# The phases of a head pair in another order: three score tiles, half the values, three groups of turning

## The chip, the cores and the metric

The kernel runs on one core of a Trainium2 chip. What counts is the device time of one execution in microseconds (us). The engines are named TensorE (PE in the rows), VectorE (DVE), ScalarE (ACT), GpSimd (POOL) and SyncE (SP, which here issues most DMAs).

## The reference

Causal attention by blocks of 64 positions, then a layer of eight experts of which each token takes one:

```python
scores = q @ k.T / sqrt(64)                     # q, k, v: (8 batches, 8 heads, 576, 64)
scores = where(block_i >= block_j, scores, -1e9)  # blocks of 64 positions
attn = exp(scores - max); attn /= sum(attn) + 1e-9
x = (attn @ v), heads side by side              # (4608, 512)

logits = x @ w_gate                             # 8 experts
e_idx = argmax(logits)
out = softmax(logits)[e_idx] * sigmoid(x @ w_output_gate)[e_idx] * (relu(x @ w1[e_idx]) @ w2[e_idx])
```

## The kernel before, in words

The first 355 us or so are attention, the rest the experts. Attention goes through 32 pairs of heads (8 batches of four pairs). The 576 positions of a head make five query tiles, four of 128 and a last one of 64. A pair has three phases, and they belong to three different pairs at a time: `attend` issues the scores of pair p, the turning of pair p-1 and the values of pair p-2, a piece of each in turn.

- `softmax` (lines 321 to 402) is a generator with four steps. Step one computes the scores of query tiles 0 and 1 into one PSUM tile (`ps_s`, two buffers of two banks), steps two and three those of tiles 2 and 3, step four the last tile of both heads together. A step is score matmuls (L345, three passes over 16-bit halves of q and k; L392 for the last tile), small matmuls that add the mask (L353), row maxes on VectorE (L364, with a raised priority) and exps on ScalarE (L357, L398). I write S01, S2, S3 and SL for them.
- `flip` (L411 to L445) turns the probabilities, because the second product needs keys on the partitions. It has seven steps, F1 to F7, each up to four transposes on TensorE (L417) into one bank of `ps_t` (three banks, used in turn by everything that is called `ps_t`) and one copy out of it. The copies go to VectorE (L437 for F1 and F4, L444 for F7) and to ScalarE (L437 for F2, F3 and F5, L441 for F6).
- `values` (L447 to L475) has two steps, V1 and V2: half the key tiles each (L457, into the one bank `ps_a`); V2 ends with the last query tile (L470) and the copies into `xT` (L464, L474).

When the last values of a batch are out, `finish_batch` (L479 on) is put on the list `later`, and each "tick" takes one step of it. Four ticks come to a pair. Ticks 1 to 4: sums and their reciprocals (L482 on), the gate's logits (L512, twice), nothing. Ticks 5 to 8: `rows(LAST)` (transposes back L495, normalising L498 on VectorE, a DMA to DRAM), transposing logits (L527), L537 with a chain of VectorE operations (L538, L544 twice, L545, L550 to L561) and `rows(0)`. Ticks 9 to 12: `rows(1)` to `rows(3)`, then the ranks within an expert (L569 to L588), whose result `sli` the scatters of GpSimd (L607) wait for.

`others` runs beside it, one step per quarter of a pair: loads of the next batch, the splitting of q and k into halves on GpSimd (`split_qk`, L143 to L150, for pair p+2) and, in the first quarter, the transposing DMA of pair p+1 (`turn_qk`, L159).

The order on TensorE is the order in which `attend` issues, as the body stands in a block `manual_schedule`; between one pair's block and the next one's the scheduler may still move matmuls. The other engines' orders are made by the scheduler from priorities and readiness. Before the change a pair is issued in four quarters: a score step, in the second and fourth quarter a value step, then two, one, two and two turning steps, `others`, and a tick.

Of the kernel before, what the change touches and what calls it, by code (L numbers as in the profile page):

```python
# [26 lines left out]
def block_attention_top1_moe(  # L27
# [12 lines left out]
    B, H, S, D = q.shape  # L40
# [244 lines left out]
    later = []  # L285
# [125 lines left out]
    def flip(probs, pT):  # L411


        def group(srcs):
            ps = ps_t.tile([P, 512], F32, name="ps_t")
            for i, src in enumerate(srcs):
                nc.tensor.transpose(ps[:, P * i:P * i + P], src, ident)  # L417
            return ps

        def slots(j0, n, t, w):  # L420
            x = turned_at(j0, t)
            if n == 1:
                return pT[:, x:x + w]
            d = turned_at(j0 + 1, t) - x
            return pT[:, x:x + d * n].rearrange("p (j c) -> p j c", c=d)[:, :, 0:w]

        def keys(pt, j):
            return pt[:, P * j:P * j + P]

        def both(t, j):  # L430
            return [keys(probs[t][:, ab], j) for ab in range(2)]

        for (t, j0, j1), to in zip(((1, 0, 2), (2, 0, 2), (2, 2, 3), (3, 0, 2), (3, 2, 4)), "vssvs"):
            n = j1 - j0
            ps = group([x for j in range(j0, j1) for x in both(t, j)])
            o, x = slots(j0, n, t, 256), ps[:, 0:256 * n]
            copies[to](o, x if n == 1 else x.rearrange("p (j c) -> p j c", c=256))  # L437
            yield
        pl = probs[LAST]
        ps = group([pl[:, S0:S0 + P], *both(0, 0)])  # L440
        copies["s"](pT[:, S0:S0 + 3 * P], ps[:, 0:3 * P])  # L441
        yield
        ps = group([keys(pl, j) for j in range(4)])
        copies["v"](pT[:, 0:S0], ps)  # L444
        yield  # L445

    def values(hp, pT, vv, vl, xT):  # L447

        a0 = 2 * hp
        pa = ps_a.tile([P, 512], F32, name="ps_a")  # L450
        for j0, j1 in ((0, 2), (2, LAST)):
            for j in range(j0, j1):
                for ab in range(2):
                    o = slice(64 * ab, 64 * ab + 64)
                    x = turned_at(j, j)
                    m = LAST - j
                    nc.tensor.matmul(  # L457
                        pa[o, P * j:S0].rearrange("p (t n) -> p t n", n=P), vv[:, j, a0 + ab],
                        pT[:, x:x + 256 * m].rearrange("p (t n) -> p t n", n=256)[:, :, P * ab:P * ab + P],
                        start=(j == 0), stop=(j == LAST - 1),  # L460
                    )
            if j0 == 0:
                yield
        nc.scalar.copy(xT[:, hp, 0:S0], pa)  # L464
        pm = ps_t.tile([P, 512], F32, name="ps_t")
        for j in range(NT):
            for ab in range(2):
                o = slice(64 * ab, 64 * ab + 64)
                x = 64 * ab + turned_at(j, LAST)
                nc.tensor.matmul(  # L470
                    pm[o, 0:64], vv[:, j, a0 + ab] if j < LAST else vl[:, a0 + ab], pT[:, x:x + 64],
                    start=(j == 0), stop=(j == LAST),
                )
        nc.vector.tensor_copy(xT[:, hp, S0:S], pm[:, 0:64])  # L474
        yield  # L475
# [192 lines left out]
    def sequence(order, i0, used):  # L668
        seq = []
        for i, kind in enumerate(order):  # L670
            k = KINDS.index(kind)
            seq.append((BKIND[k] + used[k], 2 - k, i0 + i))
            used[k] += 1
        return seq
# [4 lines left out]
    extra = sequence(rest, len(steps), used)  # L679
# [311 lines left out]
    def step(g, n=1):  # L991
        for i in range(n):
            next(g, None)

    def attend(soft, extra=None):

        nxt, flipped, valued = [], iter(()), iter(())
        if flips:
            hp, b, probs, sums, xT, vab = flips.pop()
            pT = sb.tile([P, NPT], F32, name="pT")  # L1000
            nxt = [(hp, b, pT, vab, sums, xT)]
            flipped = flip(probs, pT)
        if prods:
            hp, b, pT, vab, sums, xT = prods.pop()
            valued = values(hp, pT, *vab, xT)
        else:
            hp = None
        with tc.manual_schedule(engines=ENG):
            for r in range(4):
                step(soft)  # L1010
                if r % 2:
                    step(valued)
                step(flipped, (2, 1, 2, 2)[r])
                if extra is not None:
                    extra(r)
                for g in list(later):
                    if next(g, later) is later:
                        later.remove(g)
        if hp == NP - 1:
            later.append(finish_batch(b, *sums, xT))  # L1020
        prods.extend(nxt)

    w1b, w2b, xg, fetching = [], [], [], []
    for p in range(NPR):
# [32 lines left out]

        probs = {}
        attend(softmax(p, *sums, probs), others)
        flips.append((hp, b, probs, sums, xT, values_of[b]))  # L1060
        if p == CP:
# [16 lines left out]
    def both_x(r):  # L1078
        if r > 1:
            stage_x(steps[0], (r - 2, r - 1))  # L1080

    attend(iter(()), both_x)
    hp, b, pT, vab, sums, xT = prods.pop()
    ended = values(hp, pT, *vab, xT)
# [121 lines left out]
```

## Time and profile before

| | |
|---|---|
| three timed runs, median | 800.64 us (798.12 to 802.45) |
| the profiled execution's own time | 793.01 us |
| its span, first to last instruction | 791.1 us |
| mean granted clock of TensorE | 0.993 of full speed |
| busy share of the span | PE 94 %, DVE 68 %, ACT 61 %, POOL 44 % |

In the profile a row of a timeline gives the start of an instruction (or of several alike, with their count behind x), its duration, the line, the operation, output tile <- input tiles and their shapes; a bracket at its end is the idle time of the engine before it and what ended that. Matmuls are pipelined, so that one starts before the last one's duration is over; what a step takes is read from start to start.

### The profile page before, as it was taken

How to read it: one execution, taken by the hardware profiler on the slowest of the kernel's cores; microseconds unless marked ns; L12 is line 12 of the kernel's file. 1: busy time of each engine (PE TensorE's matmuls, PEld its weight loads, DVE VectorE, ACT ScalarE, POOL GpSimd, SP SyncE). 2: the span in 40 equal slices, each digit the busy share in tenths (PEclk: the TensorE clock that was granted, in tenths of full speed). 3: DMA queues.
4: the chain of work that ended last, by engine and by line, in shares of the span. 5: the costliest groups of instructions: out<-in, count | busy, mean ns of one | idle time of the engine just before them, and what ended most of it. 6: DMA issues, size and time to landing. Idle time of an engine off the chain costs nothing. (4 is left out here: it accounts for less than half of the span.)

```text
span 791.1 us, 18769 instructions
## 1 busy us (share of the span) xinstructions
PE 746.1 (94%) x7159; PEld 524.4 (66%) x7182; DVE 539.4 (68%) x946; ACT 480.6 (61%) x1065; POOL 346.3 (44%) x341
## 2 busy tenths in 40 slices
PE   6999998999999999996999999999999999999994
PEld 4777776777666776664847666766667666666662
DVE  6766878778786978776675865755678555785530
ACT  5777675767767576773245665755577555765530
POOL 4295486584949395544435621422223223200001
PEclk9999999999999999999999999999999999999998
DMA  6989999999999949355945589575989769621601
GB/s 170 169 171 168 227 147 177 163 134 209 151 213 145 183 96 170 65 164 162 227 106 140 152 283 259 155 240 147 282 270 299 183 203 271 162 58 49 233 28 42
DMA packets 238352, 135.92 MB, mean 172 GB/s; under 512 B 194096, under 2 KB 210544, under 8 KB 238256
## 3 DMA queue, kind: packets, MB, share of 16 engines
q1 hardware_dynamic: 229440, 115.11, 65.5%
q0 software_dynamic: 8272, 19.29, 7.9%
q8 instruction: 58, 0.95, 0.5%
q14 instruction: 38, 0.31, 0.2%
q10 hardware_dynamic: 544, 0.26, 0.1%
HBM read 122.23 MB, written 19.73 MB: 179 GB/s over the span
## 5 line engine op out<-in xcount | busy, mean ns | idle before, releaser
L949 PEld LDWEIGHTS <-w1b 128*128 128x128 f16 (+1 forms) x2112 | 182.6, 98 | 28.8 <-issue 5.9
L949 PE MATMUL ps_s<-xt,w1b 128*128 128x256 f16 (+3 forms) x1824 | 182.1, 261 | 0.5 <-DVE w1b L833 0.4
L976 PE MATMUL ps_t<-w2b,hh 128*128 128x512 bf16 (+1 forms) x585 | 175.9, 379 | 0.0
L833 DVE TENSOR_TENSOR w2b<-w2f,w2b 128x1024 bf16<-128x1024 f32 x76 | 88.0, 1220 | 113.6 <-ACT w2b L832 113.6
L364 DVE TENSOR_REDUCE nmx<-ps_s 128x1 f32<-128x512 f32 (+4 forms) x224 | 130.2, 614 | 35.9 <-PE ps_s L353 32.0
L357 ACT ACTIVATE pt<-ps_s,nmx 128x256 f32<-128x256 f32 (+3 forms) x256 | 132.2, 531 | 17.2 <-DVE nmx L364 14.8
L980 POOL DMA_INDIRECT out_dram<-ys,ids x38 | 43.3, 1139 | 178.9 <-ACT ys L979 116.3
L976 PE MATMUL ps_t<-w2b,hl 128*128 128x512 f16 x304 | 115.2, 379 | 1.5 <-DVE hl L958 0.4
L417 PE MATMUL ps_t<-ident,pt 128*128 128x128 f32 x640 | 99.4, 283 | 11.1 <-ACT pT L437 7.7
L979 ACT ACTIVATE ys<-ps_t,ids 128x512 f32<-128x512 f32 x38 | 26.1, 687 | 134.0 <-PE ps_t L976 110.0
L976 PEld LDWEIGHTS <-hh 128*128 128x128 f16 x608 | 59.2, 98 | 66.8
L417 PEld LDWEIGHTS ps_t<-ident,pt 128*128 128x128 f32 x640 | 69.5, 141 | 41.1 <-ACT pT L437 9.4
L437 ACT COPY pT<-ps_t 128x512 f32<-128x512 f32 (+1 forms) x96 | 49.5, 516 | 65.6 <-PE ps_t L417 65.6
L833 DVE TENSOR_TENSOR w1b<-w1f,w1b 128x1024 bf16<-128x1024 f32 x76 | 88.3, 1218 | 0.3 <-ACT w1b L832 0.3
L457 PE MATMUL ps_a<-pT,vv 128*64 128x256 f32 (+3 forms) x512 | 83.3, 446 | 0.0
L607 POOL DMA_INDIRECT tab_d<-idg,sli x40 | 40.1, 1003 | 89.6 <-DVE sli L588 67.2
L345 PE MATMUL ps_s<-qk 64*128 64x256 f16 (+1 forms) x1152 | 70.7, 253 | 7.8 <-DMA qk<-sp 5.3
L832 ACT CAST w1b<-w1f 128x1024 f16<-128x1024 f32 x76 | 73.9, 1044 | 1.2 <-DMA w1f<-in_moe_w_dram 1.2
L832 ACT CAST w2b<-w2f 128x1024 f16<-128x1024 f32 x76 | 73.6, 1043 | 0.0
L804 POOL DMA_INDIRECT xg<-x_d,ids x38 | 53.1, 1399 | 45.1 <-DMA ids<-tab_d 13.6
L143 POOL TENSOR_SCALAR natq<-natq 128x640 f32<-128x640 f32 x28 | 51.0, 1822 | 34.1 <-DVE pT L437 25.6
L345 PEld LDWEIGHTS <-qk 64*128 64x128 f16 x1152 | 44.0, 94 | 31.0 <-issue 20.3
(192 smaller groups left out, 1043.5 us busy)
## 6 DMA issues: line engine op xcount, KB each, us to landing
w1f<-in_moe_w_dram SPq DMA_DIRECT2D x76, 512.0 KB
w2f<-in_moe_w_dram SPq DMA_DIRECT2D x76, 512.0 KB
vv<-in_v_dram SPq DMA_DIRECT2D x64, 128.0 KB
x_d<-xn SPq DMA_DIRECT2D x32, 256.0 KB
natk<-in_k_dram SPq DMA_DIRECT2D x14, 512.0 KB
natq<-in_q_dram SPq DMA_DIRECT2D x28, 256.0 KB
hh<-in_moe_w_dram SPq DMA_DIRECT2D x4, 512.0 KB
hl<-in_moe_w_dram SPq DMA_DIRECT2D x4, 512.0 KB
```

What stands on the lines that cost most here:

```text
L143: last_pool[0] = nc.gpsimd.tensor_scalar(qv, qv, SCALE, None, ALU.mult)
L345: nc.tensor.matmul(ps[:, ab, c:c + m], qk[rows, cq, P * t:P * t + P], cols(qk[rows, ck], x, kind), start=(i == 0), stop=(i == 2 and c + m ...
L357: last_exp[0] = nc.scalar.activation(probs[t][:, ab], ps[:, ab, c0:c0 + n], AF.Exp, bias=nmx[:, t, ab:ab + 1], accum_out=sums[:, t, 2 * hp ...
L364: last_max[0] = nc.vector.tensor_reduce(o, x, AX.X, ALU.max, negate=True)
L417: nc.tensor.transpose(ps[:, P * i:P * i + P], src, ident)
L437: copies[to](o, x if n == 1 else x.rearrange("p (j c) -> p j c", c=256))
L457: nc.tensor.matmul(pa[o, P * j:S0].rearrange("p (t n) -> p t n", n=P), vv[:, j, a0 + ab], pT[:, x:x + 256 * m].rearrange("p (t n) -> p t n ...
L804: nc.gpsimd.indirect_dma_start(out=xg[i % NXG][:, h], out_offset=None, in_=x_d[0:nx, :], in_offset=IOA(ap=ids[i][:, h, 0:1].bitcast(U32), ...
L832: nc.scalar.copy(hi, src)
L833: eng.tensor_tensor(lo, src, hi, ALU.subtract)
L949: nc.tensor.matmul(ph[:, f4].rearrange("p (h n) -> p h n", n=P), wv[:, cc, f, :], xv[:, cc], start=(k == 0), stop=(k == 3 * KD - 1))
L976: nc.tensor.matmul(py, hv[:, f, h], wv[:, f, :], start=(k == 0), stop=(k == 3 * KF - 1))
```

## The change

The four quarters are replaced by a string that is read letter by letter: S, F and V take one step of scores, turning and values, a point calls `others` for the next quarter, t is a tick.

```diff
         with tc.manual_schedule(engines=ENG):
-            for r in range(4):
-                step(soft)
-                if r % 2:
-                    step(valued)
-                step(flipped, (2, 1, 2, 2)[r])
-                if extra is not None:
-                    extra(r)
-                for g in list(later):
-                    if next(g, later) is later:
-                        later.remove(g)
+            for x in "SSV.tFFFS.tSFFV.tFF.t":
+                if x == "S":
+                    step(soft)
+                elif x == "V":
+                    step(valued)
+                elif x == "F":
+                    step(flipped)
+                elif x == "t":
+                    tick()
+                else:
+                    beside(next(turns))
```

`tick` and `beside` hold what stood in the loop. In the same letters the order before was `SFF.t SVF.t SFF.t SVFF.t`; now it is `SSV.t FFFS.t SFFV.t FF.t`. Three places show what this does to the engines' orders in the built program. Numbers tell buffers apart: `qk_1775`, for instance, is the transposed q and k of one pair; `plast2` and `pt0` are probabilities.

TensorE at the seam between two pairs, the one without ticks and the one with ticks 1 to 4; F6 and F7 of one pair and the first scores of the next. Before:

```order
L470 MATMUL ps_t_1866<-pT_1521,vlast1_106 64x64 x2
L417 MATMUL ps_t_1878<-ident_88,plast2_117 128x128
L417 MATMUL ps_t_1878<-ident_88,pt0_1526 128x128 x2
L417 MATMUL ps_t_1883<-ident_88,plast2_117 128x128 x4
L345 LDWEIGHTS qk_1775
L345 MATMUL ps_s_1895<-qk_1775 128x128
```

And now:

```order
L470 MATMUL ps_t_1861<-pT_1521,vlast1_106 64x64 x2
L417 MATMUL ps_t_1878<-ident_88,plast2_117 128x128
L417 MATMUL ps_t_1878<-ident_88,pt0_1526 128x128 x2
L345 LDWEIGHTS qk_1788
L345 MATMUL ps_s_1895<-qk_1788 128x128
L417 MATMUL ps_t_1883<-ident_88,plast2_117 128x128 x4
L345 LDWEIGHTS qk_1788
```

One score matmul of the next pair has moved ahead of F7. The order before has such a place once, the order now 21 times: after nine F6, after six L537 (five matmuls there) and after six F7 ahead of L569.

TensorE in the pair with ticks 9 to 12, where F3 is the group that writes `ps_t_1601` (from `pt2`), and the L495 are the transposes of `rows`. Before:

```order
L417 MATMUL ps_t_1550<-ident_88,pt1_1330 128x128 x4
L417 MATMUL ps_t_1556<-ident_88,pt2_1373 128x128 x4
L495 MATMUL ps_t_1568<-ident_88,xT_212 128x128 x4
...
L457 MATMUL ps_a_1596<-pT_1316,vv_710 64x512 x2
L457 MATMUL ps_a_1596<-pT_1316,vv_710 64x384 x2
L417 MATMUL ps_t_1601<-ident_88,pt2_1373 128x128 x2
L495 MATMUL ps_t_1608<-ident_88,xT_212 128x128 x4
```

And now:

```order
L495 MATMUL ps_t_1508<-ident_88,xT_212 128x128 x4
...
L457 MATMUL ps_a_1570<-pT_1316,vv_723 64x512 x2
L457 MATMUL ps_a_1570<-pT_1316,vv_723 64x384 x2
L495 MATMUL ps_t_1581<-ident_88,xT_212 128x128 x4
L417 MATMUL ps_t_1589<-ident_88,pt1_1330 128x128 x4
L417 MATMUL ps_t_1595<-ident_88,pt2_1346 128x128 x4
L417 MATMUL ps_t_1601<-ident_88,pt2_1346 128x128 x2
```

The third `ps_t` tile before F3's was F1's own (`ps_t_1550`) and is now that of `rows(1)` (`ps_t_1581`).

VectorE from the chain of tick 7 to the L498 of tick 9 (the second one below), in the first batch that has it. Before:

```order
L545 TENSOR_TENSOR L<-lh 128x80
L484 COPY sums<-sumL 64x4
L444 COPY pT<-ps_t 128x512
L550 TENSOR_REDUCE mx<-L 128x5
L498 TENSOR_TENSOR xn<-ps_t,rec 128x512
...
L364 TENSOR_REDUCE nmx<-ps_s 128x2
L558 TENSOR_TENSOR oh<-er,erev 128x40
L437 COPY pT<-ps_t 128x2x256
L561 MEMSET oh 64x4
L498 TENSOR_TENSOR xn<-ps_t,rec 128x512
```

And now:

```order
L545 TENSOR_TENSOR L<-lh 128x80
L498 TENSOR_TENSOR xn<-ps_t,rec 128x512
L550 TENSOR_REDUCE mx<-L 128x5
L364 TENSOR_REDUCE nmx<-ps_s 128x2 x2
L553 TENSOR_TENSOR eq<-L,mx 128x40
L364 TENSOR_REDUCE nmx<-ps_s 128x1
...
L578 TENSOR_REDUCE add<-oh 128x8
L597 TENSOR_TENSOR z<-L,oh 128x40
L498 TENSOR_TENSOR xn<-ps_t,rec 128x512
L437 COPY pT<-ps_t 128x2x256
```

The maxes of two score steps (L364) and most of the small operations now stand ahead of the second L498, where before there were the maxes of one step and F1's copy.

## Rows read from the trace of the kernel before

**Rows 1.** The windows of 40 us from 20 to 340 us, the first and the last of eight (the six between also have clock 1.00), and their sum. Columns: window, length, busy us and instructions in brackets of TensorE, its weight loads, VectorE, ScalarE and GpSimd; granted clock of TensorE; DMA share; GB/s.
```profile
20.00:60.00 40.00, 38.55 (x471) 28.22 (x472) 28.32 (x54) 30.94 (x102) 22.84 (x20) 1.00 0.89 170
...
300.00:340.00 40.00, 37.50 (x466) 27.35 (x466) 31.80 (x84) 26.86 (x85) 19.16 (x19) 1.00 0.59 106
sum 320.00, PE 307.10 PEld 221.73 DVE 243.92 ACT 223.61 POOL 202.18; mean PE 38.39 PEld 27.72 DVE 30.49 ACT 27.95 POOL 25.27
```
**Rows 2.** The waits of TensorE between 20 and 340 us: tile and line that waited, what for; us in total, times, longest.
```profile
PE ps_s L345 <- DMA qk<-sp: 5.3, 6, 1.5
PE ps_t L417 <- DVE pT L444: 3.0, 5, 0.8
PE ps_t L417 <- ACT pT L437: 2.6, 6, 1.0
```
**Rows 3.** TensorE's timeline for a pair with ticks 5 to 8. Columns: start, length, line, operation, tiles, count.
```profile
251.67 0.34 PE L345 MATMUL ps_s<-qk 64*128 64x128 f16 x6 [1.48 <-DMA qk<-sp]
251.85 0.19 PE L353 MATMUL ps_s<-mneg,mrow 64*128 64x64 bf16 x2
251.88 0.49 PE L345 MATMUL ps_s<-qk 64*128 64x256 f16 x6
252.21 0.19 PE L353 MATMUL ps_s<-mneg,mrow 64*128 64x64 bf16 x2
252.33 1.09 PE L417 MATMUL ps_t<-ident,pt 128*128 128x128 f32 x8
253.26 0.60 PE L495 MATMUL ps_t<-ident,xT 128*64 128x128 f32 x4
253.79 0.67 PE L345 MATMUL ps_s<-qk 64*128 64x256 f16 x12
...
254.42 1.72 PE L457 MATMUL ps_a<-pT,vv 128*64 128x512 f32 x8
256.08 0.44 PE L417 MATMUL ps_t<-ident,pt 128*128 128x128 f32 x2
...
260.93 0.33 PE L417 MATMUL ps_t<-ident,plast 128*128 128x128 f32 x1
```
**Rows 4.** The same view at two seams between pairs: in the first, one score matmul of the next pair stands among the last turning groups (two rows), in the second none does (two rows).
```profile
36.38 0.33 PE L417 MATMUL ps_t<-ident,plast 128*128 128x128 f32 x1
...
38.26 1.09 PE L417 MATMUL ps_t<-ident,pt 128*128 128x128 f32 x8
...
45.87 0.33 PE L417 MATMUL ps_t<-ident,plast 128*128 128x128 f32 x1
...
47.44 0.76 PE L417 MATMUL ps_t<-ident,pt 128*128 128x128 f32 x5
```
**Rows 5.** The same view, F3 in the pair after that of rows 3, with the wait ahead of it in brackets.
```profile
264.81 0.66 PE L417 MATMUL ps_t<-ident,pt 128*128 128x128 f32 x4 [0.78 <-DVE pT L444]
```
**Rows 6.** VectorE: two groups of its lines between 20 and 340 us (busy us, mean ns of one), then its timeline in the pair after that of rows 3.
```profile
L544 DVE TENSOR_TENSOR lh<-lh 128x320 f32<-128x320 f32 (+1 forms) x12 | 10.6, 883 | 0.6
...
L545 DVE TENSOR_TENSOR L<-lh 128x80 f32<-128x80 f32 x6 | 4.5, 746 | 0.2
...
264.08 0.67 DVE L444 COPY pT<-ps_t 128x512 f32<-128x512 f32 x1
...
264.78 0.67 DVE L498 TENSOR_TENSOR xn<-ps_t,rec 128x512 f32<-128x512 f32 x1
265.38 0.18 DVE L553 TENSOR_TENSOR eq<-L,mx 128x40 f32<-128x40 f32 x1
265.49 0.18 DVE L591 TENSOR_TENSOR d<-L,mx 128x40 f32<-128x40 f32 x1
...
265.71 0.68 DVE L364 TENSOR_REDUCE nmx<-ps_s 128x2 f32<-128x512 f32 x1
...
266.41 0.41 DVE L364 TENSOR_REDUCE nmx<-ps_s 128x2 f32<-128x256 f32 x1
...
268.29 1.01 DVE L364 TENSOR_REDUCE nmx<-ps_s 128x1 f32<-128x384 f32 x2
```
**Rows 7.** The same two lines of VectorE between 20 and 340 us by the view of one line: shortest, median and longest in ns, first and last start.
```profile
L544 DVE TENSOR_TENSOR lh<-lh x12: 316/758/1399, 85.7 to 305.0; 128x320 f32<-128x320 f32 x6, 128x160 f32<-128x160 f32 x6
...
L545 DVE TENSOR_TENSOR L<-lh x6: 241/636/1359, 87.9 to 306.4; 128x80 f32<-128x80 f32 x6
```
**Rows 8.** GpSimd's timeline: the first scatter of a batch, with the wait ahead of it.
```profile
231.95 1.06 POOL L607 DMA_INDIRECT tab_d<-idg,sli  x1 [11.18 <-DVE sli L588]
```
**Rows 9.** The end of attention: two windows of 2 us (columns as in rows 1), TensorE's timeline, ScalarE's timeline.
```profile
360.00:362.00 2.00, 1.62 (x8) 1.62 (x9) 1.53 (x2) 0.44 (x3) 2.00 (x3) 0.58 0.91 317
362.00:364.00 2.00, 2.00 (x14) 1.40 (x13) 0.99 (x2) 1.59 (x3) 2.00 (x3) 0.57 0.90 213
...
360.38 1.11 PE L417 MATMUL ps_t<-ident,pt 128*128 128x128 f32 x4 [5.08 <-ACT pT L437]
...
367.19 0.18 PE L569 MATMUL ps_t<-oh,below 128*128 128x40 f16 x1 [0.89 <-ACT pT L441]
...
371.15 0.27 PE L949 MATMUL ps_s<-xh,w1b 128*128 128x256 f16 x1 [2.00 <-ACT xh L901]
...
359.01 1.04 ACT L832 CAST w2b<-hh 128x1024 f16<-128x1024 f32 x1 [5.24 <-DMA hh<-in_moe_w_dram]
...
369.57 1.04 ACT L832 CAST w2b<-hl 128x1024 f16<-128x1024 f32 x1 [2.43 <-DMA hl<-in_moe_w_dram]
```

More of the change, by code (lines that the diff above doesn't have):

```diff
@@ L1007, in attend, with tick, beside @@
             hp = None
+        def tick():
+            for g in list(later):
+                if next(g, later) is later:
+                    later.remove(g)
+        def beside(r):
+            if extra is not None:
+                extra(r)
+        turns = iter(range(4))
         with tc.manual_schedule(engines=ENG):
-            for r in range(4):
-                step(soft)
-                if r % 2:
+            for x in "SSV.tFFFS.tSFFV.tFF.t":
+                if x == "S":
+                    step(soft)
+                elif x == "V":
                     step(valued)
-                step(flipped, (2, 1, 2, 2)[r])
-                if extra is not None:
-                    extra(r)
-                for g in list(later):
-                    if next(g, later) is later:
-                        later.remove(g)
+                elif x == "F":
[4 more added lines that the diff above has]
+                    beside(next(turns))
         if hp == NP - 1:
```

## The prediction

> **What bounds the kernel now.** I read the windows first [rows 1]. From 20 to 340 us, where attention runs from one head pair to the next, TensorE is busy for 307.10 of 320 us, and the granted clock is 1.00, its higher level, in all eight windows. So TensorE sets the time there, and two things can move the end: the work that stands on TensorE, and the 12.9 us in which it waits. The view of its waits names them [rows 2]: six waits of a score matmul (L345) for the transposing DMA of queries and keys, 5.3 us, and eleven waits of a turning group (L417) for a PSUM bank whose copy was late, 3.0 + 2.6 = 5.6 us. The experts behind 371 us are not touched by the order of a pair, apart from the seam at 355 to 371 us.
>
> I call a pair's steps S01, S2, S3, SL (score tiles), F1 to F7 (turning groups), V1 and V2 (halves of the values). Four pairs run per batch: P1 has ticks 1 to 4 of finish_batch (tick 4 does nothing), P2 ticks 5 to 8, P3 ticks 9 to 12, P4 none. The DMA waits fall between P1 and P2.
>
> **The change, part by part.** No instruction is added or removed. What moves is counted in four terms.
>
> A. Changes between kinds of matmul. The timeline of TensorE shows the price [rows 3]: a score (251.88) starts 0.03 us after a small mask matmul (251.85), which is laid out on the array alike; a turning transpose (252.33) starts 0.12 us after one (252.21). The difference, 0.09 us, is a change of kind. A plain pair has 9 changes before and 7 after, as S01 S2 and F1 F2 F3 now stand together; over the program, finish_batch's matmuls included, I count 78 fewer: 78 x 0.09 = -7.0 us. Against that stands something that the string doesn't say: the built order pulls the first score matmuls of the next pair in among the last groups, 20 times more than before. The kernel before does it once, and the trace shows what it takes [rows 4]: from F6 to the first group after S01 38.26 - 36.38 = 1.88 us, against 47.44 - 45.87 = 1.57 us in the usual order. 0.31 us each, 20 x 0.31 = +6.2 us. A = -0.8 us; bounds -7.0 (the one row is chance) and +1.
>
> B. Banks. Of the 5.6 us of bank waits, which fall in P2 and P3 of six batches (one is in [rows 5], 0.78 us of F3 for the copy of F7's tile), I expect none at its old place: two score tiles and half the values now lie between F7 and F1. In P3 one comes instead. ps_t has three banks in turn, so F3 takes the bank of the third tile before it; that is now tick 9's rows(1), which the normalising L498 on VectorE must have read, and L498 stands behind a long file there.
> TensorE first. P2 from 251.67 to 260.93 holds, in another order, the same steps as the new P2 up to the end of V2 and L537 [rows 3]: 9.26 us. From there to F3 stand the pulled-in scores .2, F6 and F7 .9 (seven transposes, where eight take .93), rows(0) .53, the rest of S01 .5, S2 .63, V1 1.66 and rows(1) .53, F1 F2 .93: 5.9 us. F3 could start at 15.1.
> VectorE starts L538 when L537's result is there, at about 9.4. By the rows of the present order [rows 6], each less the .07 by which one starts before the last has ended, come then L538 .27; L544 twice and L545, 2 x .883 + .746 = 2.51; L444 .60; rows(0)'s L498 .60; L550 .1; two maxes of S01 .61 + .34; two of S2 .94; eight small ones of .11; rows(1)'s L498 .60. Sum 7.4, so the bank is free at 16.8: a wait of 1.7 us, in six batches 10.2 us. B = 10.2 - 5.6 = +4.6 us. The bounds come from the same three additions: with the shortest of the trace, .32 + .32 + .24 = 0.9 [rows 7], nothing is waited for (B = -5.6), with the longest, 4.2, each wait is 3.3 us (B = +14). I take the mean.
>
> C. The DMA waits. Their chain begins with sli (L588): GpSimd's scatter waited 11.18 us for it and starts at 231.95 [rows 8], then four more scatters and the splits of two pairs stand in its queue, and TensorE's wait for the transposes of the second ends at 251.67 [rows 3]. That is 20 us, across P4 and P1, and the change touches none of it. P4 and P1 lose four changes of kind (4 x .09 = .36 us) and get one or two pulled-in scores (.31 to .62 us), so TensorE comes to the wait at its old distance. C = 0; bounds -5.3, where P2's scores always come later than the transposes, and +2.2, where the .36 us of six batches are waited away.
>
> D. The end. At 355.3 TensorE runs out: a bank of F3's, copied by ScalarE (L437) behind L832, which waits for hh until 359.01. That costs 5.08 us, and after it the clock is granted at .58, the lower level, in the two windows up to 364 [rows 9]: 4 x (1 - .575) = 1.7 us more. Both stay, since F2's and F3's copies still stand behind that L832. What moves is the copy L441 that L569 waits for: in ScalarE's new order it is behind the fourth L832 (369.57), in the old one ahead of it. So L569 (367.19) and behind it the first half of the last values (1.72 us, as at 254.42 [rows 3]) come out of the gap before L949 (371.15, after 2.00 us of waiting) and are put behind it: about +1.9 us with L569's own .2; bounds 0 and +4 (the seam's clock once more).
>
> The waits of VectorE and ScalarE are under TensorE's cover: they are busy for 243.92 and 223.61 of the 320 us [rows 1]. The score tiles don't lose cover either: between S01 and S3, which takes over its banks, stand F1 F2, S2, V1 and F3 in both orders, and between S2 and SL stand V1, two groups, F3 and S3. If VectorE's new order makes a max late all the same, it costs tenths a pair; the range has room for that.
>
> Sum: -0.8 + 4.6 + 0 + 1.9 = +5.7 us. The profiled execution took 793.0 us (span 791.1), so 798.7 as profiled. The median of the three timed runs, 800.64, is 7.6 above it; the same sum on that is 806.3, and I say 806.
>
> **Rivals.** First, no net change: F3's wait doesn't come. L544 and L545 run as at the lower end of [rows 7], because the splits on GpSimd no longer lie beside them, and L498 is in time. Then B is -5.6, the sum -4.5; with half of the batches so, +0.6 and 801. For it: the lengths of these additions differ by four times from one batch to another. Against: both the splits and P2's scores wait for the same transposes, so they keep their places to each other.
>
> Second, faster: TensorE falls behind GpSimd. If P4 and P1 together run a microsecond later than the queue that starts with sli, the transposes land before the scores ask, and the splits of P2 are through before L544. The DMA waits, 5.3 us in six [rows 2], shrink by 4.4 (each by one microsecond or to nothing), of which P4 and P1 pay some 3 themselves; F3's wait goes too: -0.8 - 5.6 - 1.4 + 1.9 = -5.9 us, 794.7. It decides where P4 and P1 have grown by about 1 us. Against: I count no growth there, and the 20 us of queue [rows 8] don't move.
>
> Third, the clock. In the trace every window with bank waits of up to a microsecond still had 1.00 [rows 1, 5]; only the stop of 5.08 us was followed by the lower level [rows 9]. Should F3's waits of 1.7 us be enough for it, each batch pays the seam's 1.7 us, 6 x 1.7 = 10.2, and the time is 816.
> The Trainium skill, TensorE: Matmul & The Clock Gate, section "A second HAM failure mode: psum-queue depth-cycling", has a kernel in which TensorE idled between groups as it went round its PSUM banks and the clock swung between its levels. By that rule the third case is the one to expect; this trace, which goes round three banks with eleven waits at 1.00, doesn't bear it out.
>
> **How the numbers follow.** The forecast has .47, with 801 to 813 as its own range. No net change has .25, faster .23, the clock .05. A measurement of this kernel can tell about 0.5 %, 4 us, from no change. Faster (under 796.6): .22, the second rival but for its upper edge. Same (796.6 to 804.6): .30, the first rival and the lower edge of the forecast. Slower: .48, the rest. Eight in ten lie between 794, where the second rival stands, and 813.
>
> **What would show it.** A: TensorE's timeline has S2 straight behind S01's masks at .03, and single scores among F6, F7 and L569. B: among TensorE's waits L417 waits for VectorE at F3 of P3, once a batch, 0.2 to 3.3 us, and none is left at the old places. C: six L345 waits for qk of some 5 us in all. D: L569 starts after the fourth L832. The prediction is wrong if TensorE's idle time between 20 and 340 us doesn't grow by some 4.6 us, if F3 doesn't wait, or if TensorE's busy time there falls by several microseconds because the pulled-in scores cost nothing.

## The result: 1.0 % slower

The changed kernel takes 806.2 us (median of six runs, 804.2 to 807.8), the kernel before beside it 798.1 us (six runs): a ratio of 1.0104, 95 % interval 1.0064 to 1.0144, or some 8 us. A second set of four runs of the same kernel gave 803.7 us against 792.4, 1.0146 (1.0107 to 1.0185). The profiled execution of the first set took 806.4 us with a span of 804.7, that of the second 799.9 with 798.3; before it was 793.0 with 791.1 [rows 1 and the table above].

The windows answer to [rows 1]; the columns are the same. They show the fifth of eight, whose busy time has fallen most, and the sum:

```profile
180.00:220.00 40.00, 35.13 (x409) 24.87 (x407) 26.95 (x65) 26.01 (x87) 25.29 (x23) 0.96 1.02 163
...
sum 320.00, PE 301.37 PEld 221.24 DVE 239.26 ACT 216.26 POOL 200.91; mean PE 37.67 PEld 27.65 DVE 29.91 ACT 27.03 POOL 25.11
```

TensorE is now idle for 18.6 us of the 320, 5.7 more than before (16.6 in the second set's profile, 3.7 more), and the granted clock is no longer 1.00 in every window. What TensorE waits for, in the same stretch, answers to [rows 2]:

```profile
PE ps_t L417 <- DVE xn L498: 8.8, 6, 2.4
PE ps_s L345 <- DMA qk<-sp: 5.2, 3, 2.2
PE ps_t L417 <- DVE xT L474: 1.6, 2, 0.8
```

The eleven waits of L417 for L437 and L444 are gone, but for 0.3 us, and six waits for L498 stand in their place, one in each of six batches. One of them on TensorE's timeline, in the pair with ticks 9 to 12 (columns as in [rows 3]):

```profile
136.94 0.66 PE L495 MATMUL ps_t<-ident,xT 128*128 128x128 f32 x4
137.43 1.04 PE L417 MATMUL ps_t<-ident,pt 128*128 128x128 f32 x8
140.12 0.44 PE L417 MATMUL ps_t<-ident,pt 128*128 128x128 f32 x2 [1.65 <-DVE xn L498]
```

The x2 group is F3. TensorE is through with F1 and F2 1.04 us after their start and then stands for 1.65 us. The VectorE timeline of another batch shows the file that it waits for:

```profile
224.81 0.27 DVE L538 TENSOR_TENSOR lh<-ps_t,rec 64x128 f32<-64x128 f32 x1
225.18 0.85 DVE L544 TENSOR_TENSOR lh<-lh 128x320 f32<-128x320 f32 x2
...
226.72 0.68 DVE L498 TENSOR_TENSOR xn<-ps_t,rec 128x512 f32<-128x512 f32 x1
...
227.42 1.01 DVE L364 TENSOR_REDUCE nmx<-ps_s 128x2 f32<-128x512 f32 x2
...
230.32 0.69 DVE L498 TENSOR_TENSOR xn<-ps_t,rec 128x512 f32<-128x512 f32 x1
```

From L538 to the end of the second L498, 6.2 us, VectorE stands still for no more than about 0.1 us at a time, and the additions (L544 and L545, .85 and .23) are short here. In this batch F3 waits only 0.52 us; in others, where they are longer, up to 2.38.

Four points in TensorE's timeline divide the span: the first F6 of all, F6 in the last attend that has scores, the first matmul of the experts (L949), and the end.

| | before | changed, first set | changed, second set |
|---|---|---|---|
| first F6 | 25.16 | 28.27 | 28.28 |
| F6 in the last attend with scores | 348.93 | 356.70 | 352.98 |
| first L949 | 371.15 | 381.57 | 376.28 |
| end of the span | 791.1 | 804.7 | 798.3 |

The start up to the first F6 takes 3.1 us more in both, attention from there on 4.7 and 0.9 more, the seam 2.7 and 1.1 more, the experts 3.2 and 2.1 more.

From the first F6 to the last one of the table TensorE has the same pieces of work in either order, so its busy time there can be compared (in a window of fixed length more waiting alone makes it smaller). The windows, before and then the second set:

```profile
25.16:348.93 323.77, 311.73 (x3772) 225.01 (x3770) 246.86 (x555) 225.22 (x723) 205.21 (x185) 1.00 0.89 162
```

```profile
28.28:352.98 324.70, 308.47 (x3761) 226.71 (x3762) 245.61 (x554) 223.80 (x726) 207.49 (x187) 1.00 0.84 160
```

TensorE is busy for 3.3 us less and stands for 16.2 us instead of 12.0. In the first set's profile it is 310.17 us, of which 1.7 are a stretch at the lower clock: 308.5 again.

**The start.** The 3.1 us up to the first F6 are mostly waits. TensorE's rows that waited for over half a microsecond between 10 us and there, with F6 itself; first before, then the second set:

```profile
13.01 0.83 PE L345 MATMUL ps_s<-qk 64*128 64x256 f16 x12 [0.64 <-ACT pt L357]
16.89 0.34 PE L345 MATMUL ps_s<-qk 64*128 64x128 f16 x6 [1.36 <-ACT pt L357]
23.78 0.33 PE L174 MATMUL ps_t<-ident,natq 128*128 128x128 f32 x1 [0.87 <-ACT pT L437]
25.16 0.31 PE L417 MATMUL ps_t<-ident,plast 128*128 128x128 f32 x1
```

```profile
13.52 0.83 PE L345 MATMUL ps_s<-qk 64*128 64x256 f16 x12 [1.67 <-ACT pt L357]
18.54 0.34 PE L345 MATMUL ps_s<-qk 64*128 64x128 f16 x6 [1.77 <-ACT pt L357]
22.34 0.44 PE L417 MATMUL ps_t<-ident,pt 128*128 128x128 f32 x2 [0.81 <-DVE pT L437]
24.59 1.09 PE L177 MATMUL ps_t<-ident,natk 128*64 128x128 f32 x16 [1.01 <-ACT pT L437]
28.28 0.30 PE L417 MATMUL ps_t<-ident,plast 128*128 128x128 f32 x1
```

5.3 us instead of 2.9. The first attend has no turning and no values and the second no values, so less stands between two score tiles there, which would explain the waits. Another 0.4 us are six score matmuls that are pulled in ahead of this F6, a place that the list in the section on the change doesn't have.

**The clock.** Before, one stretch of TensorE's timeline is granted the lower level [rows 9], but for the last 8 us of the span, in which TensorE has next to nothing left to do. In the changed kernel there are five, at 18, 214, 368, 378 and 420 us, each of about 1.7 us in lost work. The windows around two of them, and the instruction ahead of the first:

```profile
212.92 0.34 PE L345 MATMUL ps_s<-qk 64*128 64x128 f16 x6 [2.24 <-DMA qk<-sp]
```

```profile
214.00:216.00 2.00, 2.00 (x14) 0.70 (x10) 1.71 (x4) 1.10 (x5) 1.92 (x3) 0.55 1.27 218
216.00:218.00 2.00, 2.00 (x12) 0.77 (x9) 0.00 (x0) 1.75 (x8) 2.00 (x2) 0.60 1.66 180
...
378.00:380.00 2.00, 1.82 (x10) 0.75 (x11) 1.35 (x3) 0.61 (x2) 0.00 (x0) 0.51 0.00 0
380.00:382.00 2.00, 2.00 (x10) 0.64 (x7) 1.06 (x5) 0.00 (x0) 0.55 (x1) 0.64 0.00 0
```

2 x (.45 + .40) = 1.7 us for the first. Not every stretch costs that: with the one at 18 us the first F6 starts at 28.27, in the second set without it at 28.28, so it fell into time that is waited away. The other three more than before are 5.1 of the 13.4 us by which this execution is longer than the profiled one of before. The second set's profile has two stretches, at 362 and 372 us, one more than before, and is 6.9 us longer. Over the ten runs of the changed kernel the mean granted clock is .981 to .987 and once .992; over the nine of before beside the second set it is .986 to .992. The means, .985 and .989, differ by 0.004; times 795 us that is an estimate of some 3 us, and an upper one, as part of it falls into waits.

### The profile page after: what moved, and what is told of

It reads as the page before. It is cut to its first block, busy times and chain, and to the rows that moved or that the text cites. A ratio compares the mean times of both kernels' runs of the same rounds, so it can differ in the third digit from the quotient of the medians.

```text
span 804.7 us, 18860 instructions
## 1 busy us (share of the span) xinstructions
PE 752.5 (94%) x7182; PEld 529.6 (66%) x7182; DVE 538.4 (67%) x946; ACT 479.1 (60%) x1065; POOL 344.0 (43%) x341
## 5 line engine op out<-in xcount | busy, mean ns | idle before, releaser
L949 PEld LDWEIGHTS <-w1b 128*128 128x128 f16 (+1 forms) x2112 | 182.5, 98 | 25.6 <-issue 2.6
L949 PE MATMUL ps_s<-xt,w1b 128*128 128x256 f16 (+3 forms) x1824 | 182.1, 261 | 0.3 <-DVE w1b L833 0.2
L976 PE MATMUL ps_t<-w2b,hh 128*128 128x512 f16 x608 | 181.8, 381 | 0.0
L364 DVE TENSOR_REDUCE nmx<-ps_s 128x1 f32<-128x512 f32 (+4 forms) x224 | 127.1, 616 | 24.1 <-PE ps_s L353 19.7
L417 PE MATMUL ps_t<-ident,pt 128*128 128x128 f32 x640 | 92.1, 281 | 13.1 <-DVE xn L498 11.1
L457 PE MATMUL ps_a<-pT,vv 128*64 128x256 f32 (+3 forms) x512 | 86.6, 461 | 1.2 <-ACT pT L441 1.2
L417 PEld LDWEIGHTS ps_t<-ident,pt 128*128 128x128 f32 x640 | 72.1, 144 | 22.0 <-DVE xn L498 12.7
L832 ACT CAST w1b<-w1f 128x1024 f16<-128x1024 f32 x76 | 73.9, 1044 | 0.2 <-DMA w1f<-in_moe_w_dram 0.2
L832 ACT CAST w2b<-w2f 128x1024 f16<-128x1024 f32 x76 | 73.6, 1042 | 0.0
L804 POOL DMA_INDIRECT xg<-x_d,ids x38 | 50.7, 1335 | 50.7 <-issue 14.8
L345 PEld LDWEIGHTS <-qk 64*128 64x128 f16 x1152 | 48.9, 95 | 24.1 <-issue 11.8
L957 ACT ACTIVATE hh<-ps_s 128x1024 f16<-128x1024 f32 (+1 forms) x44 | 39.9, 906 | 28.9 <-PE ps_s L949 24.2
```

The lines of the kernel that those rows point to most:

```text
L345: nc.tensor.matmul(ps[:, ab, c:c + m], qk[rows, cq, P * t:P * t + P], cols(qk[rows, ck], x, kind), start=(i == 0), stop=(i == 2 and c + m ...
L364: last_max[0] = nc.vector.tensor_reduce(o, x, AX.X, ALU.max, negate=True)
L457: nc.tensor.matmul(pa[o, P * j:S0].rearrange("p (t n) -> p t n", n=P), vv[:, j, a0 + ab], pT[:, x:x + 256 * m].rearrange("p (t n) -> p t n ...
L804: nc.gpsimd.indirect_dma_start(out=xg[i % NXG][:, h], out_offset=None, in_=x_d[0:nx, :], in_offset=IOA(ap=ids[i][:, h, 0:1].bitcast(U32), ...
L832: nc.scalar.copy(hi, src)
L949: nc.tensor.matmul(ph[:, f4].rearrange("p (h n) -> p h n", n=P), wv[:, cc, f, :], xv[:, cc], start=(k == 0), stop=(k == 3 * KD - 1))
```

## The experiments

Each ratio is against the kernel before in its own set of runs. The waits are TensorE's from 20 to 340 us.

| run | median, us | ratio (95 %) | waits that matter |
|---|---|---|---|
| control (the changed kernel) | 803.7 | 1.0146 (1.0107 to 1.0185) | L498 10.7 |
| rows_late | 811.5 | 1.0236 (1.0200 to 1.0272) | L437 at L495 12.0 |
| no_pull | 800.8 | 1.0112 (1.0063 to 1.0161) | L498 13.1 |
| end_before | 800.1 | 1.0083 (1.0054 to 1.0112) | L498 11.4 |
| one_sum | 794.6 | 1.0043 (1.0017 to 1.0069) | L498 6.7 |
| one_sum_before | 788.0 | 0.9972 (0.9945 to 0.9998) | L437 2.4 |
| ss_only | 799.8 | 1.0112 (1.0067 to 1.0158) | L498 at L470 6.9 |
| combo | 792.7 | 1.0034 (1.0006 to 1.0062) | L498 7.9 |
| small_late | 803.7 | 1.0138 (1.0106 to 1.0169) | L498 at L470 8.6, at L417 3.9 |
| end_after | 793.2 | 1.0006 (0.9987 to 1.0025) | as before |
| all5 | 793.5 | 1.0004 (0.9987 to 1.0021) | L498 at L470 6.8 |
| best_before | 786.3 | 0.9922 (0.9894 to 0.9950) | none of L417 |

**The changed kernel again.**

> The changed kernel once more, as the measure for the others and to see which of its stretches at the lower clock come back. Theory (four extra stretches at the lower clock, each behind a long wait of TensorE, are part of the price): 804 to 808 us, the stretches at the seam (about 368, 378 and 420 us) come back, the one at 214 us, behind a DMA wait of 2.24 us, need not. Rival (these stretches are chance): another number of them at other places, time spread by several us.

The seam's low stretches came back (362 and 372 us), the one at 214 did not, and neither did those at 18 and 420. In the four runs the time goes from 799.9 us at a mean clock of .992 to 806.4 at .982. So stretches at the lower clock are part of the price, but of those outside the seam an execution gets some and not others. Without them the two profiles agree: the first F6 comes at 28.27 and 28.28 us, and the work between the two F6 takes 308.5 us of TensorE in both.

**Another tile for F3's bank.** The tick moves behind F1 F2 F3, so that F3 takes over `rows(0)`'s bank:

```diff
-            for x in "SSV.tFFFS.tSFFV.tFF.t":
+            for x in "SSV.FFFtS.tSFFV.tFF.t":
```

> The first tick of a pair stands behind F1 F2 F3 instead of ahead of them, so that F3 takes over rows(0)'s bank and not rows(1)'s. Theory (bank of rows(1)): the six waits of L417 for L498, 8.8 us in the profile, go but for some tenths; 8 us faster than the changed kernel, about 798. Rival 1 (the time behind the waits comes back as DMA waits of L345, since P2 and P3 only get ahead of the queue on GpSimd): waits for qk rise by 5 us or more and at most 3 us are gained. Rival 2 (VectorE is late all the same, and F4 or F5 waits instead): 6 us or more of L417 waits for VectorE remain, no gain.

8 us slower instead of 8 faster. The waits for L498 at L417 are gone, and the waits view has this instead:

```profile
PE ps_t L495 <- DVE pT L437: 12.0, 12, 2.7
PE ps_t L417 <- ACT pT L437: 2.4, 5, 0.6
```

`rows(1)` now comes third behind F1 and waits for F1's copy, which stands in VectorE's file where L498 stood. The second rival is the right one, at an earlier place than it named: the bank only decides which instruction is caught; VectorE is late. Six of the twelve waits, one a batch, are of 0.74 to 2.67 us; the other six, at `rows(LAST)`, are of 0.20 us each. That is 1.3 us more than the control's waits for L498, so they alone don't explain the 8 us. Behind three of them (2.67, 1.87 and 1.82 us) the profile has a stretch at the lower clock; the rest is open.

**Nothing pulled in.** The scores of step one are issued after the last matmul of the pair before (`last_pe`, which is set behind each turning group, `rows` and the rank matmul):

```diff
...
-            scores(pX, t, c0)
+            with tc.issue_after(last_pe[0].ins) if last_pe[0] else nullcontext():
+                scores(pX, t, c0)
...
```

> The scores of step one may not be issued ahead of the last turning group, rows transposes or rank matmul of the pair before, so no score matmul is pulled in; nothing else changes. Theory (a pulled-in score costs 0.2 to 0.3 us each time): 9 x 0.30 + 12 x 0.2 = 5 us of TensorE's busy time, and about 3 to 5 us of the time, as those ahead of F3's wait and of a DMA wait give theirs to the wait. Rival (all of it is eaten by waits that end at the same time): 0 to 1 us gained, and the waits grow by what the matmuls lose.

What a pulled-in score costs can be read in the changed kernel itself, from F6 to V1, first without and then with one:

```profile
39.78 0.33 PE L417 MATMUL ps_t<-ident,plast 128*128 128x128 f32 x1
...
41.88 1.08 PE L457 MATMUL ps_a<-pT,vv 128*64 128x512 f32 x4
```

```profile
48.70 0.33 PE L417 MATMUL ps_t<-ident,plast 128*128 128x128 f32 x1
...
49.18 0.23 PE L345 MATMUL ps_s<-qk 64*128 64x128 f16 x1
49.34 0.66 PE L417 MATMUL ps_t<-ident,plast 128*128 128x128 f32 x4
...
51.10 1.08 PE L457 MATMUL ps_a<-pT,vv 128*64 128x512 f32 x4
```

2.10 against 2.40 us: 0.30, as forecast from one place. From the first F6 to the last with scores the window without them is

```profile
27.97:353.61 325.64, 306.10 (x3767) 225.32 (x3767) 249.58 (x555) 222.46 (x722) 205.51 (x186) 0.99 0.82 159
```

It holds one stretch at the lower clock, behind F3's wait at 140 us; less its 1.7 us TensorE is busy for 304.4 us, 4.1 less than the control's 308.47. So the pulled-in scores cost 4.1 us in all, 0.2 each. But TensorE stands for 19.5 us instead of 16.2: the waits for L498 rise from 10.7 to 13.1 us and those for L474 from 0.9 to 2.3. The median falls by 2.9 us, and the intervals of the two ratios overlap. Both expectations are half right: the matmuls lose 4 of the 5 us, and in the profile 3.3 of these are waited away.

**The old order in the last attend, and the new one there alone.**

```diff
+    p_last = [True]
...
-            for x in "SSV.tFFFS.tSFFV.tFF.t":
+            for x in "SSV.tFFFS.tSFFV.tFF.t" if p_last[0] else "SFF.tSVF.tSFF.tSVFF.t":
...
+    p_last[0] = False
     attend(iter(()), both_x)
```

> The last attend, which has no scores, keeps the order before the change; the other 32 have the new one. Theory (the seam costs 4 us by L441 behind the last L832 and the low clock behind its longer waits): L569 comes before the fourth L832, the first L949 comes 3 to 5 us earlier, one or two stretches at the lower clock at the seam go, 4 to 7 us gained in all. Rival (the seam is set by the DMAs of the weights, hh and hl, which come 6 us later because attention ends later): L949 moves by less than 1 us.

3.6 us by the medians, and the intervals just touch. From F6 in the last attend with scores to L949 it takes 20.12 us instead of the control's 23.30.

> The kernel before with the new order in the last attend alone, the counterpart of the run with the old order there. Theory (the seam's price is the order of the last attend): from the last score tile to the first L949 some 28 us instead of 24.4, 3 to 5 us slower than the kernel before, a second stretch at the lower clock at the seam. Rival (the price comes from attention ending later): within 1.5 us of the kernel before.

The counterpart costs 0.06 %, nothing that can be told from no change. Its seam is longer in the profile (24.75 us instead of 22.22), but the time isn't. So the order of the last attend is worth something in the changed kernel and next to nothing in the old one; my price for it doesn't stand by itself.

These two runs also place the start. With the old order in the last attend alone the first F6 comes at 28.54 us; with the new order there alone it comes at 25.22. In all ten profiles with score tiles in pairs at the beginning it comes at 28.0 to 29.0 us, in the four others at 25.2 (once 26.8). And they show how far two executions of the same order differ: from the first F6 to the last with scores this run has the order of the kernel before and TensorE is as busy (311.76 and 311.73 us), but it stands for 9.0 us instead of 12.0, as its waits for qk are 2.5 us and not 5.3.

**A shorter file.** One reduction takes the place of three additions; the sum is the same, in another order of adding:

```diff
-        for w in (4, 2):
-            nc.vector.tensor_tensor(lh[:, :, 0:w], lh[:, :, 0:w], lh[:, :, w:2 * w], ALU.add)
-        nc.vector.tensor_tensor(L, lh[:, :, 0], lh[:, :, 1], ALU.add)
+        nc.vector.tensor_reduce(L, lh.rearrange("p t h c -> p t c h"), AX.X, ALU.add)
```

> The changed kernel, with the three additions over the heads (L544 twice and L545, 2.5 us of VectorE in a row) made one reduction of 640 numbers a row (the row max over 576 takes 0.75 us). Theory (F3 waits for the end of VectorE's file, whichever tile is late): each F3 wait shrinks by about 1.7 us, the L417 waits for L498 fall from 9 to 11 us to under 2, and the time by 6 to 9 us against the changed kernel. Rival (the L498 waits for something else, its rows transposes or a DMA's buffer): waits stay within 2 us and the time within 2 us.

The ratio falls from 1.0146 to 1.0043, 8 us, at the upper end of the expectation. The wait shrinks less than expected, as the reduction itself is longer than I had taken it; the lines and waits views show

```profile
L543 DVE TENSOR_REDUCE L<-lh 128x80 f32<-128x640 f32 x6 | 7.6, 1262 | 0.7
```

```profile
PE ps_t L417 <- DVE xn L498: 6.7, 6, 1.4
```

1.26 us and not 0.75. Longest wait 1.4 instead of the control's 2.5 us: taking work off VectorE helps where moving it didn't. The waits account for 4 of the 8 us. The mean granted clock, .989 over these ten runs and .985 over the control's four, would be some 3 us by the same estimate as above; that it is the rest isn't shown.

> The same reduction in the kernel before. Theory (there it is F7's copy L444 behind the additions that F3 waits for, 3.0 us in five): those waits go, 2 to 3 us gained and the waits for ScalarE (2.6 us) and qk stay. Rival (a shorter file on VectorE is worth as much there as in the changed kernel, so the additions are no part of the difference between the two): 6 us or more gained.

2.2 us (0.9972, the interval just off one), as expected. By the ratios the same reduction is worth three to four times as much in the new order, where it stands ahead of an instruction for which TensorE waits up to 2.5 us.

**Only the score tiles together**, F1 and F2 ahead of the values again:

```diff
-            for x in "SSV.tFFFS.tSFFV.tFF.t":
+            for x in "SSFF.tVFS.tSFFV.tFF.t":
```

> Score tiles in pairs, but F1 and F2 ahead of the first half of the values and F3 behind it: SSFF.t VFS.t SFFV.t FF.t. Theory (what costs is V and the tick between the scores and F1, which put rows(1)'s L498 and F1's copy behind two steps' maxes): the L498 waits at F3 fall to under 4 us; one change of kind a pair more than the changed kernel (32 x 0.09 = 2.9 us); 3 to 7 us faster than the changed kernel. Rival (two score steps in a row alone fill VectorE's file): waits for VectorE of 8 us or more remain in that batch's pair, time within 3 us.

No better than the changed kernel by more than the intervals allow. Waits for VectorE remain, at two new places: V2's L470 for an L498 (6.9 us in six) and L417 for F1's copy (3.6 in six). The rival held: two score steps in a row are enough, as far as this order can tell, in which S3 and SL still stand together too.

**Moving the small operations.** They are pinned behind `rows(1)`'s L498 (`last_rows`) and issued in the tick that follows it, so that `rows(0)` and `rows(1)` now come ahead of them:

```diff
...
+        yield
+        if not rush:
+            for t in range(2):
+                rows(t)
+                yield
+
         mx = small.tile([P, NT], F32, name="mx")
-        nc.vector.tensor_reduce(mx, lg, AX.X, ALU.max)
+        with tc.issue_after(last_rows[0].ins) if last_rows[0] else nullcontext():
+            nc.vector.tensor_reduce(mx, lg, AX.X, ALU.max)
...
```

> The changed kernel, with the eight small VectorE operations of tick 7 and after (mx, eq, er, oh and what follows from them) pinned behind rows(1)'s L498 instead of ahead of it; the maxes of S01 and S2 stay ahead. Theory (F3 waits for the sum of what stands in VectorE's file): each F3 wait shrinks by the eight times 0.11 us, 0.9 us, so the L498 waits fall from about 10 us to 5, and 3 to 6 us are gained against the changed kernel. Rival (the maxes alone set it, the small ones run in their gaps): waits unchanged within 1.5 us. A second one (sli comes later and with it GpSimd's queue): waits for qk rise by 4 us or more.

F3's waits fall, from 10.7 to 3.9 us, and the time doesn't:

```profile
PE ps_t L470 <- DVE xn L500: 8.6, 6, 1.5
PE ps_t L417 <- DVE xn L500: 3.9, 5, 1.3
```

(L500 here is L498 elsewhere.) V2's L470 now waits for `rows(2)`'s L498. None of the expectations named that. The windows of the pair with ticks 9 to 12, F6 to L569, say why; first before, then the changed kernel:

```profile
129.95:143.67 13.72, 12.58 (x141) 9.20 (x138) 12.77 (x35) 8.29 (x27) 2.92 (x4) 1.00 1.13 222
```

```profile
132.86:146.66 13.80, 12.10 (x133) 9.20 (x133) 12.29 (x35) 7.85 (x26) 2.19 (x3) 1.00 1.04 221
```

The fourth number is VectorE: 12.77 of 13.72 us and 12.29 of 13.80. Its share is .93 and .89, TensorE's .92 and .88: it is as full as TensorE in this pair. That what is taken ahead in its file is missing behind follows from this, but is not shown apart. From 20 to 340 us as a whole it is busy for three quarters, which hides this.

**All repairs together.** `combo` is the new order with no pulling-in, the old order in the last attend and the reduction; `all5` has the pinning as well.

> The changed kernel with the three repairs together: no score matmuls pulled in, the order before in the last attend, one reduction in place of three additions. Theory (the price is the sum of these three: F3's file, pulled-in scores, seam): 7.0 us of changes of kind are left over as a gain and the bank waits of the kernel before are gone too; 5 to 11 us faster than the kernel before. Rival (the saved time comes back as DMA waits, since GpSimd's queue of 20 us from L588 on sets P4 and P1): L345 waits for qk above 8 us and at most 3 us faster than the kernel before.

> The new order with all repairs: nothing pulled in, the old order in the last attend, one reduction, and the small operations behind rows(1)'s L498. Theory: the F3 waits fall to 2 or 3 us in all, and the saved changes of kind are left: 785 to 790, 1 to 5 us faster than the kernel before. Rival (the gain of the changes of kind goes into the DMA waits between P1 and P2): waits for qk of 5 us or more, and no faster than the kernel before.

Neither beats the kernel before: 1.0034 and 1.0004. `combo` can't be told from the reduction alone (1.0043): the two repairs that gained 2.9 and 3.6 us by themselves add nothing that shows. Its window between the two F6 tells where the gain went:

```profile
28.27:348.81 320.54, 304.22 (x3767) 224.36 (x3767) 242.70 (x543) 223.37 (x722) 204.09 (x186) 1.00 0.84 161
```

TensorE is busy for 304.22 us, 7.5 less than in the kernel before: the changes of kind are saved, as forecast. It stands for 16.3 us (12.0 before, 9.0 in `end_after`), and the start takes 3.1 us. The last F6 comes at 348.81 us, in the kernel before at 348.93. In `all5` the waits for qk are 3.4 us, so the gain didn't go there; the L470 wait for L498 6.8 us and F6 waits for L474 3.8 us.

**The same repairs in the old order:**

> The kernel before with the reduction and the small operations behind rows(1)'s L498. Theory (in the old order F3 there waits for ScalarE's copy, not for VectorE's file): no more than 1 us beyond what the reduction alone gave there, 787 to 789. Rival (a shorter file is worth as much in either order): 784 or less.

786.3 us, 0.9922 (0.9894 to 0.9950): the fastest of all, 6 us ahead of the kernel before. The number lies between what theory and rival said, but the kernel before stood at 793.15 us in this set and at 790.75 in the one from which they were reckoned. By the ratios it is 4 us beyond the reduction alone, where the theory allowed 1; the rival is nearer. So the later place of the small operations in VectorE's file gains something in the old order, if hardly clear of noise (the intervals, 0.9894 to 0.9950 and 0.9945 to 0.9998, just overlap), and why isn't shown: no run has them alone there. No turning group waits for a bank any more; the two largest of TensorE's waits are

```profile
PE ps_s L345 <- DMA qk<-sp: 2.6, 2, 2.2
PE ps_t L174 <- ACT pT L437: 0.9, 1, 0.9
```

The windows between the two F6 of `all5` and `best_before`, which have the same repairs for VectorE:

```profile
28.44:351.53 323.09, 305.04 (x3767) 224.82 (x3767) 241.10 (x543) 223.62 (x726) 206.37 (x187) 1.00 0.85 160
```

```profile
26.78:341.84 315.06, 310.34 (x3772) 225.69 (x3770) 242.62 (x543) 224.98 (x723) 203.95 (x185) 1.00 0.85 166
```

The new order gives TensorE 5.3 us less to do and lets it stand for 18.1 us instead of 4.7. By the medians, taken beside each other, it is 7.3 us slower.

## Why the prediction was right, and where it was not

The direction, the place of the waits and the term for them were right; the size, +5.7 us, was smaller than the 8 us of the first set and the 11 of the second. That the median came out at the forecast number owes something to the kernel before, whose median fell by 2.5 us when more runs were taken.

The start was put at nothing, and that step failed. I read the windows from 20 us on and argued that the score tiles lose no cover, as F1, F2, V1 and F3 stand between them in either order. In the first attend no F and no V stand there, in the second no V, and the first F6 comes 3.1 us later in both profiles. That the new order causes this is shown by `end_before` and `end_after`; that it is the missing F and V is argued from the order.

A, changes of kind and pulled-in scores, -0.8: on the same work TensorE's busy time fell by 3.3 us. The changes of kind were right (`combo` has 7.5 us less where 7.0 were forecast). The pulled-in scores were put at the price of the one row that I had, 0.31 us each and 6.2 in all; that price is right for a place like it (0.30), but all of them together cost 4.1. What failed besides is adding this term to the time at its full size: `no_pull` takes 4.1 us off TensorE's work, of which 3.3 are waited away, and `all5`, where nothing is pulled in, should have kept the 7.0 us and kept none. My sign for it, that TensorE's busy time from 20 to 340 us should not fall, was no test, as in 320 us it must fall by what the waits rise.

That the waits of VectorE are under TensorE's cover I had read from its share of the 320 us, three quarters; in the pair that has F3's wait the share was .93 before the change.

B, the bank waits, +4.6: right. Forecast were six waits of 1.7 us, 10.2 in all; measured 8.8 and 10.7 in the two profiles. All old ones are gone, as forecast. The first profile's additions were shorter than those of [rows 6], and so were its waits; the same lines:

```profile
L544 DVE TENSOR_TENSOR lh<-lh 128x320 f32<-128x320 f32 (+1 forms) x12 | 9.4, 781 | 0.8
...
L545 DVE TENSOR_TENSOR L<-lh 128x80 f32<-128x80 f32 x6 | 2.7, 443 | 0.0
```

2 x .781 + .443 = 2.0 us instead of 2.5. The bounds by the additions held too: waits from 0.52 to 2.46 us. The reason that I gave, the turn of the banks, was only half of it. `rows_late` shows that another tile in that bank brings another wait; what can't be moved away is VectorE's work. In two of the six batches of the first set F3 waited for only 0.52 us, with .85 us for both L544: there the first rival was half right.

C, the DMA waits, 0: 5.2 us in three in one profile and 0.6 in one in the other, before 5.3 in six. The second profile's are smaller than the forecast, the first has two of over 2 us. In `end_after`, which has the order of the kernel before up to the last attend, they are 2.5 us in three. So no effect of the change shows, and how they fall differs from execution to execution.

D, the seam, +1.9: measured 2.7 and 1.1. L441 stands behind the fourth L832, and L569 and the half values behind it, as forecast; the rows of both engines, which answer to [rows 9]:

```profile
365.04 0.44 PE L417 MATMUL ps_t<-ident,pt 128*128 128x128 f32 x2 [2.26 <-DVE xn L498]
...
367.99 1.97 PE L417 MATMUL ps_t<-ident,pt 128*128 128x128 f32 x8 [1.70 <-ACT pT L437]
...
378.18 0.19 PE L569 MATMUL ps_t<-oh,below 128*128 128x40 f16 x1 [2.84 <-ACT pT L441]
```

```profile
376.70 1.04 ACT L832 CAST w2b<-hl 128x1024 f16<-128x1024 f32 x1 [2.80 <-DMA hl<-in_moe_w_dram]
377.65 0.47 ACT L441 COPY pT<-ps_t 128x384 f32<-128x384 f32 x1
```

That the stop of 5.08 us stays was wrong: in its place are 2.26 us for L498 and 1.70 for L437, the wait for L441 has grown from 0.89 to 2.84, and L949's 2.00 are gone. The clock fell twice here, where before it fell once. I had that as the upper bound and not in the sum.

The missing part is the start, 3.1 us, and the clock. Without both, the first set's profile is 5.4 us longer than that of before and the second's 2.4, where 5.7 were forecast. The third rival got .05 and had the price right, 1.7 us each, but only F3's waits as its place. In the first profile none of F3's six waits was followed by the lower level; a DMA wait, the start, the seam and a load of the experts were. In `end_before` three of F3's waits were followed by it. So it is not six falls or none, but some at each execution. For the tail behind L949, 2 to 3 us longer, only the stretch at 420 us (behind a wait of 2.52 us for a load) is shown, in one profile; the rest is open, as that part takes 419.4 to 423.5 us in these profiles, and longest in `best_before`, which has the old order.

## What to carry to other kernels

Look at the busy share of the engine that empties the banks in the stretch in question, not over the whole: here it was .93 in one pair of four and three quarters over all. An order that saved the matmul engine 5 to 7 us of work gained nothing, and two orders that moved the late instruction away met the wait again at another place; what helped was to take work off that engine, here a reduction for three additions. Look also at the first and the last rounds by themselves, where pieces are missing that cover a wait elsewhere. And count what the scheduler makes of a new order at its seams, as the string doesn't show it.

## What was not expected of the hardware

Waits of equal length were followed by the lower clock and not: in `end_before` F3's wait of 2.45 us at 139.82 was, its wait of 2.46 at 322.44 was not. Nor was the changed kernel's DMA wait of 2.04 us at 259.68, where that of 2.24 us at 212.92 was. The first, in the timeline and the windows, and the row of the second:

```profile
139.82 0.56 PE L417 MATMUL ps_t<-ident,pt 128*128 128x128 f32 x2 [2.45 <-DVE xn L498]
```

```profile
138.00:140.00 2.00, 0.18 (x2) 0.18 (x2) 1.91 (x9) 2.00 (x10) 0.00 (x0) 1.00 1.07 222
140.00:142.00 2.00, 2.00 (x17) 1.16 (x17) 1.23 (x8) 1.14 (x6) 0.00 (x0) 0.50 1.35 242
```

```profile
322.44 0.44 PE L417 MATMUL ps_t<-ident,pt 128*128 128x128 f32 x2 [2.46 <-DVE xn L498]
```

And a reduction on VectorE of 640 numbers that lie apart in SBUF into 80 sums took 1.26 us, the one of 576 in a row of PSUM into one maximum 0.75. Which of the differences costs the time isn't shown.
